# Sums written in place, an earlier place for joint product 2, joint product 4 for four column pairs, and a new timetable for the sequence sums

## The chip, the cores and the metric

One core of one Trainium2 chip. TensorE (PE) multiplies, VectorE (DVE) and ScalarE (ACT) do the elementwise work, SyncE (SP) and GpSimd (POOL) issue transfers. The metric is the device time of one execution in microseconds (us).

## The reference

Two results of one input x (2048 x 512) are mixed row by row with a sigmoid gate: a Fourier mixing over both axes, and a gated MLP with ReLU.

```python
def reference(A_x, dft_seq_re, dft_seq_im, dft_hid_re, dft_hid_im, W_gate, W_up, W_down, gate_w):
    g = sigmoid((x * gate_w).sum(-1, keepdims=True))
    a = einsum("bsd,ed->bse", x, dft_hid_re)
    b = einsum("bsd,ed->bse", x, dft_hid_im)
    y = einsum("ts,bse->bte", dft_seq_re, a) - einsum("ts,bse->bte", dft_seq_im, b)
    gate, up = x @ W_gate, x @ W_up          # 512 -> 1792 columns
    h = gate * (gate > 0) * up
    return g * y + (1 - g) * (h @ W_down)
```

## The kernel before

All products are in fp32, made of three fp32r matmuls each (high part by low part, low by high, high by high, the `PARTS`), 128x128 weights against 512 columns. Each 2x2 block product is a Strassen-Winograd scheme of seven products, numbered 1 to 7; the sums it needs are made by DVE, ACT makes high parts and copies out of PSUM, DVE makes low parts. In a tile's name the last letter tells the part: `xh`/`xl` and `wah`/`wal` are a high and a low part. The buffers' names in the profile have lost their numbers.

The stages on PE, in order: **gate and up** (the two start pairs of columns c = 0, 1, then c = 2, then the `Joined` pairs c = 3 to 6; 0 to about 233 us), the spectral blocks with the rest of gate and up, **Down** (two halves q of the rows, 347 to 481 us), and the **sequence stage** (26 products in the order `TURN`, each with four parts, to the end). A pair c does both row halves q = 0 and q = 1. Its seven block products use four PSUM banks x, m, y, t (`BANK`).

In `Joined` pairs product 2 (and from pair `FOURS` on product 4 too) is not made for each q on its own. `JointW` makes both q at once with seven products of a quarter of the size each ("joint product 2" and "joint product 4"; `step(y)` is three matmuls). Its steps stand between the block products, at the places that the dictionaries `slots` (joint product 2, called `joint`) and `fours` (joint product 4, called `self.four`) name: after block product m, half i. Joint product 2 gathers its results in bank x, joint product 4 in bank t; DVE and ACT bring them to `jo`, and their partial results to `jv`, `jv6`. A q's results are finished as sums (`added`, `last`): a DVE sum of PSUM and SBUF into a buffer `u`, then a `h`, the product of its rectified first half with its second half, and `h` goes to DRAM (`hd`), for some blocks with further sums `hs` (`h_sums`), for those in `RAW` without them (then `Down.made` makes them later, from the loaded blocks).

No order is written down for the other engines. Every operation is recorded with a key, a place in PE's count of matmuls, and `Plan.order` lists DVE, ACT, SP and POOL by it, from estimated times. Each engine then works strictly in its list's order, so an instruction that waits holds back all behind it. SBUF is 51 units of 4 KB per partition (`UNITS`). A buffer takes a unit whose former owner is done by the plan; on the chip its first writer waits until the last reader of the former owner, an engine or a transfer, has ended.

In the sequence stage `walk` and `Sequence.sides` decide when operands (`r` on the right, `l` on the left) are loaded and summed, split into `ch`, `cl` and `wh`, `wl`; the lead of each step before its use is `LEAD`, with a start ramp `RAMP`. Some operands (`FORMED`) are summed ahead of that stage: `form_stored` by POOL transfers DRAM to DRAM (`td`), the second of which adds, `form_rights` by DVE with loads and stores of SP (`rt`). The outputs' sums are `js`.

All instructions are recorded by one line of a helper, so every row of the profile says L267.

Of the kernel before, what the change touches and what calls it, by code (L numbers as in the profile page):

```python
# [11 lines left out]
OP = mybir.AluOpType  # L12
# [6 lines left out]
NT, KD, KF = S // N, D // P, F // P  # L19
HD = D // 2  # L20
UNITS = 51
FOURS, FOUR_KEY, FOUR_W = 4, -100, 40

# [29 lines left out]
        (25, 1), (0, -1), (4, -1)),  # L55
}

FORMED = (16, 18, 19, 28, 35, 37, 38)
DRAWN = {39: 38, 33: 16, 41: 19, 31: 2, 29: 15, 20: 15, 27: 7, 25: 7, 21: 6, 40: 9, 43: 9}
FLIP_T, FLIP_K = (1, 1, -1, -1), (1, 1, 1, 1)  # L60
LFORMED = (8, 9, 10, 11, 14, 15, 20, 21)
# [2 lines left out]
DIRECT, PLACE = (9, 10, 11, 14, 15, 20, 21), (0, 2, 3, 1)  # L64
GROUP = {9: 1, 10: 0, 11: 1, 14: 1, 15: 0, 20: 0, 21: 0}
ROOM = {'r': 6, 'l': 4}
LEAD = {'r': {'load': 56, 'sum': 56, 'sums': 8, 'draws': 30, 'hi': 42, 'lo': 34}, 'l': {'load': 40, 'sum': 46, 'sums': 8, 'draws': 56, 'hi': 55, 'lo': 48}}
RAMP = 50
FORM_LEAD = 43


def walk(side, blocks, room, ready=(), drawn={}):
# [197 lines left out]
class Plan:  # L270
# [14 lines left out]
    def op(self, key, f, *a):  # L285
        self.ops.append((key, len(self.ops), f, a))
# [135 lines left out]
def kernel(ctx: ExitStack, tc, xP, xG, wgu, wd, cr, ci, wri, gw, out):  # L422
# [24 lines left out]
    plan = Plan()  # L447
    op, pe = plan.op, plan.pe
# [6 lines left out]
    od = Buf(plan, "od", (NT, P, KD, N), kind="dram", tile=out)  # L455
    td = hbm("td", len(FORMED), 2, 2, P, 2, N)
    gd = hbm("gd", 2, NT * KD, P)
# [8 lines left out]
    def buf(name, shape=(2, N), dtype=F32):  # L466
        return Buf(plan, name, list(shape), dtype)
# [21 lines left out]
    def E():  # L489
        return plan  # L490
# [118 lines left out]
    FORM = {1: 0, 2: 1, 3: 2, 5: 3, 7: 4, 6: 5, 4: 6}  # L609


    RAW = {(0, 1), (1, 2), (0, 0), (0, 3), (0, 2), (1, 3)}

    def h_sums(q, c, h, key):
        f = [buf(f"hs{n}") for n in range(2)]
# [19 lines left out]
    def h_out(q, c, h, key):  # L635
        if (q, c // 2) not in RAW:
            h_sums(q, c, h, key)
        op(key + 2, lambda: put(hd[q, 0, :, c], h[0][:, 0]))
        op(key + 3, lambda: put(h_forms(q, c, 1), h[1].all))
        if (q, c // 2) in RAW:  # L640
            op(key + 2, lambda: put(hd[q, 3, :, c], h[0][:, 1]))

    class Block:


        def __init__(self, q, w, banks=PAIRS):
            self.q, self.w, self.banks = q, w, banks
            self.x = {m: X[q, m] for m in ORDER if (q, m) in X}
            self.g = {r: buf("g" + r, (N,)) for r in ("11", "21")}
            self.s = {m: buf(f"s{m}") for m in (5, 6)}  # L650
            self.u = {r: buf("u" + r) for r in ("12", "22")}
            self.h = [buf(f"h{d}") for d in range(2)]

        def run(self):
# [48 lines left out]


        def added(self, r, a, b, key):
            u, h = self.u[r], self.h[int(r[0]) - 1][:, int(r[1]) - 1]
            op(key, lambda: E().vector.tensor_add(u.all, a.all, b.all))
            op(key + 1, lambda: E().vector.scalar_tensor_tensor(h, u[:, 0], 0.0, u[:, 1], op0=OP.max, op1=OP.mult))

    class Joined(Block):  # L710


        def __init__(self, q, w, four=None):
            super().__init__(q, w)
            self.four = four
            if four and q:
                self.banks = {**PAIRS, "y": PAIRS["t"]}
            self.u["11"] = buf("u11")
            if four:
                self.u["21"] = buf("u21")  # L720
            if not q:
                self.s[1] = buf("s1")

        def run(self, joint=None):
            slots = {(5, 1): (5, 1), (6, 1): (6,), (3, 0): (3, 7), (3, 1): (2, 4)}
            order = [(3, 0), (7, 0), (3, 1), (7, 1), (4, 0), (4, 1)]
            fours = {}
            if self.four:
                slots = {(5, 1): (5, 1), (6, 1): (6,), (7, 0): (3, 7), (3, 0): (2, 4)}
                fours = {(6, 0): (5, 1), (7, 0): (6,), (7, 1): (3, 7), (3, 0): (2, 4)}  # L730
                order = [(7, 0), (7, 1), (3, 0), (3, 1)]
            for m, i in [(m, i) for m in (1, 5, 6) for i in range(2)] + order:
                pe(6, self.product, m, i)
                if m == 6 or m == 7 and not self.four:
                    self.half(m, i, plan.now)
                if i:
                    self.evac(m, plan.now)
                for j, some in ((self.four, fours), (joint, slots)) if joint else ():
                    for y in some.get((m, i), ()):
                        j.step(y)  # L740
                        if j is self.four and y == 4:
                            self.last(plan.now)
                if self.four and not joint and (m, i) == (7, 1):
                    self.last(plan.now)

        def last(self, key):
            u, y, o = self.u["21"], self.banks["y"], self.four.o[self.q]
            op(key + 1, lambda: E().vector.tensor_sub(u.all, y.all, o.all))
            op(key + 2, lambda: E().vector.scalar_tensor_tensor(
                self.h[1][:, 0], u[:, 0], 0.0, u[:, 1], op0=OP.max, op1=OP.mult))  # L750

        def done(self, key, joint):
            self.added("11", self.s[1] if self.q == 0 else self.banks["x"], joint.o[self.q], plan.now)
# [330 lines left out]
    class Down(Round):  # L1084
# [10 lines left out]
        def rights(self):  # L1095
            for (x, jj), key in self.at.items():
                if (self.q, jj) not in RAW:
                    raw = buf("hr")
# [27 lines left out]

    PAIRED = {v: n for n, v in enumerate(FORMED)}

# [6 lines left out]
    def formed(side, blocks, trails, parts, first, last, source, name, shape):  # L1135
# [4 lines left out]
        for part, trail in chains:  # L1140
            old = None
            for x, v in trail:
                b = buf(name, shape)
                op(key - FORM_LEAD, lambda b=b, x=x, part=part: load(b.all, source(part, x)))
                if old:
# [15 lines left out]
    def form_rights(values, first, last):  # L1161
        formed("r", 16, trails("r", 16, values), range(4), first, last, right_of, "rt", (2, N))
# [10 lines left out]
    def form_stored(values, first, gap):  # L1173

        for n, (v, part) in enumerate((v, part) for v in values for part in range(4)):
            a, b, _ = SUMS["r"][v - 16]
            if PACED:
                token(first + gap * 2 * n)
            for i, (f, x) in enumerate(((store, a), (accumulate, b))):
                op(first + gap * (2 * n + i), lambda f=f, x=x, v=v, part=part: f(right_of(part, v), right_of(part, x), max_dma_last_dim=8 * N))  # L1180

    def form_lefts(values, first, last):
        formed("l", 8, trails("l", 8, values), (0, 2), first, last, left_of, "lt", (4, HD))

    class Sequence:
# [8 lines left out]
        def ready(self, turn, part):  # L1194

            key = self.at(turn, part)
            return key - max(0, RAMP - (key - self.base) / 2)

# [66 lines left out]
        def run(self):  # L1265
            lead = LEAD["r"]
            llead = LEAD["l"]

            r = self.sides("r", 16, FORMED, DRAWN, (2, N), right_of, range(4), lead)
            l = self.sides("l", 8, LFORMED, LDRAWN, (4, HD), left_of, (0, 2), llead)  # L1270
# [253 lines left out]
    for n, m in enumerate((5, 6, 3, 7, 4)):  # L1524
        key = 24 * n + 20
        for f, *a in ((x_sum(0, m),), (hi_of, X[0, m]), (lo_of, X[0, m])):
            op(key, f, *a)
        for w in ws:
# [3 lines left out]
            else:  # L1532
                h, i = divmod(SLOT[m], 2)
# [16 lines left out]
    for b in start:  # L1550
        b.done(plan.now + 8)

    form_stored([16, 35, 37, 18], 156, 22)
    form_rights([28, 38], 864, 1253)


    spectral = Spectral()
# [6 lines left out]
    for c in range(2, NP):  # L1564
# [10 lines left out]
        else:  # L1575
            if c == FOURS:
                four_x = JointFour(plan.now + FOUR_KEY)
            four = c >= FOURS and JointW(w, four_x, plan.now + FOUR_W, 4)
# [26 lines left out]
    key = plan.now  # L1605
# [4 lines left out]
    for n in range(2):  # L1610
# [2 lines left out]
            op(key + k + 6 * n, lw.sum, m, n)  # L1613
        for m, k in ((5, -90), (6, 10), (3, 48), (7, 88), (2, 130), (4, 170)):
            lw.split(m, n, key + k + 14 * n, 8)
    form_stored([19], plan.now + 20, 25)
    Down(lw, 0)
    form_lefts([8], plan.now + -129, plan.now + 104)
    Down(lw, 1)

    Sequence().run()
# [54 lines left out]
```

## Time and profile before

| | us |
|---|---|
| median of 3 runs (768.67 to 772.97) | 770.83 |
| the profiled execution's own time | 769.49 |
| its span, first to last instruction | 767.7 |
| PE busy (3357 matmuls) | 762.1 |
| DVE busy | 677.7 |
| ACT busy | 407.8 |

The granted clock was 1.00 throughout. The profile is of one execution, 1.34 us quicker than the median; 1.8 us of its own time lie outside the span. Sums of durations are made against 769.49 and then carried to the median.

### The profile page before, as it was taken

What the parts mean: (1) busy time and instruction counts of PE and PEld (TensorE: products, weight loads), DVE (VectorE), ACT (ScalarE), POOL (GpSimd) and SP (SyncE); (2) the same over time, 40 slices, a digit from 0 to 9 for tenths busy, and PEclk for the clock granted to TensorE, in tenths of its full rate; (3) what the DMA queues carried; (4) which work ended last, traced back from release to release, by engine and by line L of the source; (5) the groups of instructions that cost most, each with busy time, mean ns of one, the idle gap of its engine ahead of it and who ended that gap; (6) DMA issues with size and microseconds to landing.
All of it is one profiled execution on the core that took longest, in us unless ns stands there. A gap on an engine that the chain in (4) does not pass through costs nothing.

```text
span 767.7 us, 9404 instructions
## 1 busy us (share of the span) xinstructions
PE 762.1 (99%) x3357; PEld 627.4 (82%) x3357; DVE 677.7 (88%) x757; ACT 407.8 (53%) x497; POOL 95.0 (12%) x118
## 2 busy tenths in 40 slices
PE   9999999999999999999999999999999999999998
PEld 7788888788788888888888888888888888888886
DVE  6999787867699885999999869998989999979987
ACT  5766454343444452656644536645674556827633
POOL 0111211112000000003510000130210210113010
PEclk9999999999999999999999999999999999999999
DMA  9385887758698999989599798998995998989984
GB/s 320 120 218 125 223 256 203 217 142 222 186 319 302 365 403 365 371 307 323 150 242 369 257 410 310 285 242 168 327 261 174 255 254 278 242 198 281 298 191 109
DMA packets 65503, 197.51 MB, mean 257 GB/s; under 512 B 6960, under 2 KB 7472, under 8 KB 65456
## 3 DMA queue, kind: packets, MB, share of 16 engines
q1 hardware_dynamic: 51776, 147.49, 52.8%
q0 software_dynamic: 13536, 49.29, 32.2%
q8 instruction: 26, 0.43, 0.2%
q14 instruction: 21, 0.17, 0.1%
q10 hardware_dynamic: 144, 0.13, 0.1%
HBM read 149.68 MB, written 68.17 MB: 284 GB/s over the span
## 4 chain that ended last, share of the span: by engine, by line
PE 88%; DVE 7%; DMA 2%; issue 2%; ACT 1%; DVEq 0%; ACTq 0%
PE ps L267 88%; DVE cl L267 2%; DVE u L267 1%; DVE r L267 1%; DMA hd<-h 1%; DMA hd<-hs 1%; DVE wl L267 1%; DVE h L267 1%; DVE js L267 0%; ACT ch L267 0%; DVE jws L267 0%; DVE wb1l L267 0%; DVE jw L267 0%; DVE jo L267 0%; DVE ps L267 0%
## 5 line engine op out<-in xcount | busy, mean ns | idle before, releaser
L267 PE MATMUL ps<-ch,wl 128*128 128x512 f32 (+1 forms) x420 | 162.7, 387 | 0.1
L267 PE MATMUL ps<-cl,wh 128*128 128x512 f32 (+1 forms) x420 | 162.7, 387 | 0.0
L267 PE MATMUL ps<-ch,wh 128*128 128x512 f32 (+1 forms) x420 | 162.5, 387 | 0.0
L267 ACT CAST ch<-r 128x1024 fp32r<-128x1024 f32 x104 | 105.3, 1052 | 95.2 <-DVE r L267 83.0
L267 DVE TENSOR_TENSOR cl<-r,ch 128x1024 fp32r<-128x1024 f32 x104 | 124.3, 1221 | 3.8 <-ACT ch L267 3.2
L267 PEld LDWEIGHTS ps<-ch,wl 128*128 128x128 f32 x420 | 78.9, 188 | 16.6 <-DVE js L267 0.5
L267 PEld LDWEIGHTS ps<-cl,wh 128*128 128x128 f32 x420 | 78.9, 188 | 16.6 <-DVE cl L267 0.4
L267 PEld LDWEIGHTS ps<-ch,wh 128*128 128x128 f32 x420 | 78.9, 188 | 15.9
L267 PE MATMUL ps<-ch,ll 128*128 128x512 f32 x196 | 76.2, 389 | 0.0
L267 PE MATMUL ps<-cl,lh 128*128 128x512 f32 x196 | 76.2, 389 | 0.0
L267 PE MATMUL ps<-ch,lh 128*128 128x512 f32 x196 | 76.2, 389 | 0.0
L267 ACT CAST ch<-hr 128x1024 fp32r<-128x1024 f32 (+1 forms) x56 | 51.0, 944 | 36.7 <-DVE hr L267 22.7
L267 ACT COPY s<-ps 128x1024 f32<-128x1024 f32 (+1 forms) x48 | 41.7, 874 | 50.1 <-PE ps L267 38.8
L267 DVE TENSOR_TENSOR cl<-hr,ch 128x1024 fp32r<-128x1024 f32 (+1 forms) x56 | 59.4, 1087 | 6.8 <-ACT ch L267 5.4
L267 POOL COPY tk<-tk 128x1 f32<-128x1 f32 x20 | 23.0, 1152 | 250.3 <-ACT tk L267 250.3
L267 ACT CAST wh<-l 128x1024 fp32r<-128x1024 f32 x38 | 39.5, 1053 | 16.3 <-DVE l L267 13.0
L267 DVE TENSOR_TENSOR wl<-l,wh 128x1024 fp32r<-128x1024 f32 x38 | 46.0, 1220 | 0.3 <-ACT wh L267 0.2
L267 PE MATMUL ps<-xh,wb0l 128*128 128x512 f32 x112 | 43.8, 391 | 0.0
L267 PE MATMUL ps<-vh,xl 128*128 128x512 f32 x112 | 43.7, 390 | 0.0
L267 PE MATMUL ps<-xl,wb0h 128*128 128x512 f32 x112 | 43.6, 389 | 0.0
L267 PE MATMUL ps<-xh,wb1l 128*128 128x512 f32 x112 | 43.6, 389 | 0.0
L267 PE MATMUL ps<-vh,xh 128*128 128x512 f32 x112 | 43.6, 389 | 0.0
(161 smaller groups left out, 1502.9 us busy)
## 6 DMA issues: line engine op xcount, KB each, us to landing
l<-ad SPq DMA_DIRECT2D x32, 512.0 KB, 7.5
hr<-hd SPq DMA_DIRECT2D x30, 512.0 KB, 6.0
r<-td SPq DMA_DIRECT2D x24, 512.0 KB, 7.4
td<-cr POOLq DMA_DIRECT2D x20, 512.0 KB, 5.2
td<-ci POOLq DMA_DIRECT2D x20, 512.0 KB, 6.0
wr<-wgu SPq DMA_DIRECT2D x16, 512.0 KB, 7.5
ad<-a SPq DMA_DIRECT2D x16, 512.0 KB, 7.4
r<-cr SPq DMA_DIRECT2D x16, 512.0 KB, 6.8
```

What stands on the lines that cost most here:

```text
L267: getattr(getattr(nc, self.engine), self.name)(*map(ap, self.a), **{k: ap(x) for k, x in self.k.items()})
```

## The change

Eight edits. (1) Sums that went to buffers `u` are written over one of their operands (`s5`, `s6`, `jo`). (2) Joint product 2's steps 2 and 4 stand right after joint product 4's steps 3 and 7, before the whole of block product 3. (3) `FOURS` is 3 instead of 4, so joint product 4 is made for pairs 3 to 6, and the keys of its operands differ. (4) `RAW` holds other blocks. (5) to (8) Other operands are summed ahead (`FORMED`), at other times, and the leads of the sequence stage differ.

```diff
--- before.py
+++ after.py
@@ -19,7 +19,7 @@
 NT, KD, KF = S // N, D // P, F // P
 HD = D // 2
 UNITS = 51
-FOURS, FOUR_KEY, FOUR_W = 4, -100, 40
+FOURS, FOUR_KEY, FOUR_W = 3, 0, 35
 
 
 
@@ -55,7 +55,7 @@
         (25, 1), (0, -1), (4, -1)),
 }
 
-FORMED = (16, 18, 19, 28, 35, 37, 38)
+FORMED = (16, 17, 18, 19, 35, 37, 38)
 DRAWN = {39: 38, 33: 16, 41: 19, 31: 2, 29: 15, 20: 15, 27: 7, 25: 7, 21: 6, 40: 9, 43: 9}
 FLIP_T, FLIP_K = (1, 1, -1, -1), (1, 1, 1, 1)
 LFORMED = (8, 9, 10, 11, 14, 15, 20, 21)
@@ -64,9 +64,9 @@
 DIRECT, PLACE = (9, 10, 11, 14, 15, 20, 21), (0, 2, 3, 1)
 GROUP = {9: 1, 10: 0, 11: 1, 14: 1, 15: 0, 20: 0, 21: 0}
 ROOM = {'r': 6, 'l': 4}
-LEAD = {'r': {'load': 56, 'sum': 56, 'sums': 8, 'draws': 30, 'hi': 42, 'lo': 34}, 'l': {'load': 40, 'sum': 46, 'sums': 8, 'draws': 56, 'hi': 55, 'lo': 48}}
-RAMP = 50
-FORM_LEAD = 43
+LEAD = {'r': {'load': 46, 'sum': 60, 'sums': 4, 'draws': 30, 'hi': 42, 'lo': 26}, 'l': {'load': 38, 'sum': 62, 'sums': 6, 'draws': 40, 'hi': 51, 'lo': 34}}
+RAMP = 80
+FORM_LEAD = 56
 
 
 def walk(side, blocks, room, ready=(), drawn={}):
@@ -609,7 +609,7 @@
     FORM = {1: 0, 2: 1, 3: 2, 5: 3, 7: 4, 6: 5, 4: 6}
 
 
-    RAW = {(0, 1), (1, 2), (0, 0), (0, 3), (0, 2), (1, 3)}
+    RAW = {(0, 1), (0, 0), (1, 1), (0, 3), (0, 2), (1, 0), (1, 3)}
 
     def h_sums(q, c, h, key):
         f = [buf(f"hs{n}") for n in range(2)]
@@ -648,7 +648,6 @@
             self.x = {m: X[q, m] for m in ORDER if (q, m) in X}
             self.g = {r: buf("g" + r, (N,)) for r in ("11", "21")}
             self.s = {m: buf(f"s{m}") for m in (5, 6)}
-            self.u = {r: buf("u" + r) for r in ("12", "22")}
             self.h = [buf(f"h{d}") for d in range(2)]
 
         def run(self):
@@ -703,9 +702,9 @@
 
 
         def added(self, r, a, b, key):
-            u, h = self.u[r], self.h[int(r[0]) - 1][:, int(r[1]) - 1]
-            op(key, lambda: E().vector.tensor_add(u.all, a.all, b.all))
-            op(key + 1, lambda: E().vector.scalar_tensor_tensor(h, u[:, 0], 0.0, u[:, 1], op0=OP.max, op1=OP.mult))
+            h = self.h[int(r[0]) - 1][:, int(r[1]) - 1]
+            op(key, lambda: E().vector.tensor_add(b.all, a.all, b.all))
+            op(key + 1, lambda: E().vector.scalar_tensor_tensor(h, b[:, 0], 0.0, b[:, 1], op0=OP.max, op1=OP.mult))
 
     class Joined(Block):
 
@@ -715,9 +714,6 @@
             self.four = four
             if four and q:
                 self.banks = {**PAIRS, "y": PAIRS["t"]}
-            self.u["11"] = buf("u11")
-            if four:
-                self.u["21"] = buf("u21")
             if not q:
                 self.s[1] = buf("s1")
 
@@ -726,7 +722,7 @@
             order = [(3, 0), (7, 0), (3, 1), (7, 1), (4, 0), (4, 1)]
             fours = {}
             if self.four:
-                slots = {(5, 1): (5, 1), (6, 1): (6,), (7, 0): (3, 7), (3, 0): (2, 4)}
+                slots = {(5, 1): (5, 1), (6, 1): (6,), (7, 0): (3, 7), (7, 1): (2, 4)}
                 fours = {(6, 0): (5, 1), (7, 0): (6,), (7, 1): (3, 7), (3, 0): (2, 4)}
                 order = [(7, 0), (7, 1), (3, 0), (3, 1)]
             for m, i in [(m, i) for m in (1, 5, 6) for i in range(2)] + order:
@@ -744,10 +740,10 @@
                     self.last(plan.now)
 
         def last(self, key):
-            u, y, o = self.u["21"], self.banks["y"], self.four.o[self.q]
-            op(key + 1, lambda: E().vector.tensor_sub(u.all, y.all, o.all))
+            y, o = self.banks["y"], self.four.o[self.q]
+            op(key + 1, lambda: E().vector.tensor_sub(o.all, y.all, o.all))
             op(key + 2, lambda: E().vector.scalar_tensor_tensor(
-                self.h[1][:, 0], u[:, 0], 0.0, u[:, 1], op0=OP.max, op1=OP.mult))
+                self.h[1][:, 0], o[:, 0], 0.0, o[:, 1], op0=OP.max, op1=OP.mult))
 
         def done(self, key, joint):
             self.added("11", self.s[1] if self.q == 0 else self.banks["x"], joint.o[self.q], plan.now)
@@ -1550,8 +1546,9 @@
     for b in start:
         b.done(plan.now + 8)
 
-    form_stored([16, 35, 37, 18], 156, 22)
-    form_rights([28, 38], 864, 1253)
+    form_stored([19, 35, 37], 181, 22)
+    form_stored([18], 810, 26)
+    form_rights([17, 38], 906, 1367)
 
 
     spectral = Spectral()
@@ -1613,9 +1610,9 @@
             op(key + k + 6 * n, lw.sum, m, n)
         for m, k in ((5, -90), (6, 10), (3, 48), (7, 88), (2, 130), (4, 170)):
             lw.split(m, n, key + k + 14 * n, 8)
-    form_stored([19], plan.now + 20, 25)
+    form_stored([16], plan.now + 112, 34)
     Down(lw, 0)
-    form_lefts([8], plan.now + -129, plan.now + 104)
+    form_lefts([8], plan.now + -149, plan.now + 98)
     Down(lw, 1)
 
     Sequence().run()
```

The first place is on PE, at the end of row half q = 0 of pair 4. `kx` are joint product 4's operands, `jx` joint product 2's (`jx2`, `jx4` for its steps 2 and 4); `xh3`, `xl3` with `wb1` are block product 3, `xh1` with `wal` is the first product of q = 1. Before:

```order
L267 MATMUL ps_76<-kx4_960,wd_1416 128x512 x3
L267 MATMUL ps_76<-jx2_665,wal_1311 128x512
L267 MATMUL ps_76<-jx2_665,wah_1284 128x512 x2
L267 MATMUL ps_76<-jx4_714,wal_1311 128x512
L267 MATMUL ps_76<-jx4_714,wah_1284 128x512 x2
L267 MATMUL ps_76<-xh3_209,wb1l_1348 128x512
L267 MATMUL ps_76<-xl3_278,wb1h_1335 128x512
L267 MATMUL ps_76<-xh3_209,wb1h_1335 128x512
L267 MATMUL ps_76<-xh3_209,wb1l_1348 128x512
L267 MATMUL ps_76<-xl3_278,wb1h_1335 128x512
L267 MATMUL ps_76<-xh3_209,wb1h_1335 128x512
L267 MATMUL ps_76<-xh1_312,wal_1311 128x512
```

Now:

```order
L267 MATMUL ps_76<-kx7_877,jw_1369 128x512 x3
L267 MATMUL ps_76<-jx2_658,wal_1295 128x512
L267 MATMUL ps_76<-jx2_658,wah_1249 128x512 x2
L267 MATMUL ps_76<-jx4_706,wal_1295 128x512
L267 MATMUL ps_76<-jx4_706,wah_1249 128x512 x2
L267 MATMUL ps_76<-xh3_209,wb1l_1358 128x512
L267 MATMUL ps_76<-xl3_278,wb1h_1303 128x512
L267 MATMUL ps_76<-xh3_209,wb1h_1303 128x512
L267 MATMUL ps_76<-xh3_209,wb1l_1358 128x512
L267 MATMUL ps_76<-xl3_278,wb1h_1303 128x512
L267 MATMUL ps_76<-xh3_209,wb1h_1303 128x512
L267 MATMUL ps_76<-xh4_361,wd_1388 128x512
```

Joint product 2's last six matmuls stood between joint product 4's last three and the second half of block product 3, six matmuls before q = 1's first. Now they stand ahead of the whole of block product 3, and 18 matmuls lie between: both its halves (12) and joint product 4's last six, of which the last row is the first.

The second place is on DVE and ACT, at the start of pair 3 (q = 0). DVE before, from the sum of product 7 on:

```order
L267 TENSOR_TENSOR u_749<-ps,s_657 128x1024
L267 TENSOR_TENSOR jw<-jws,jw 128x512
L267 TENSOR_TENSOR ws_759<-wr_612,wr_624 128x512
L267 TENSOR_TENSOR ws_759<-wr_612,ws_682 128x512
L267 TENSOR_TENSOR u_773<-ps,s_678 128x1024
L267 SCALAR_TENSOR_TENSOR h_782<-u_749 128x512
L267 TENSOR_TENSOR wb1l<-ws_759,wb1h 128x1024
L267 SCALAR_TENSOR_TENSOR h_731<-u_773 128x512
```

Now, from the same sum on, here in place in `s`; `kx` and the second `jws` and `jw` are operands of joint product 4, which pair 3 did not have:

```order
L267 TENSOR_TENSOR s_650<-ps,s_650 128x1024
L267 TENSOR_TENSOR h_730<-g_684,ps 128x512
L267 TENSOR_TENSOR wb0l<-ws_673,wb0h 128x1024
L267 TENSOR_TENSOR s_669<-ps,s_669 128x1024
L267 TENSOR_TENSOR jw<-jws,jw 128x512
```

```order
L267 TENSOR_TENSOR jx_706<-jx_666,jx_706 128x512
L267 TENSOR_TENSOR ws_761<-wr_603,wr_615 128x512
L267 TENSOR_TENSOR ws_761<-wr_603,ws_673 128x512
L267 TENSOR_TENSOR kx_772<-xs_634,xs_354 128x512
L267 SCALAR_TENSOR_TENSOR h_776<-ps,g_758 128x512
L267 TENSOR_TENSOR jws<-wr_615 128x128
L267 TENSOR_TENSOR jws<-jws,wr_615 128x128
L267 TENSOR_TENSOR jws<-wr_615 128x128
L267 TENSOR_TENSOR jws<-wr_615,jws 128x128
L267 TENSOR_TENSOR kx_780<-kx_772,kx_780 128x512
L267 SCALAR_TENSOR_TENSOR h_776<-s_650 128x512
L267 TENSOR_TENSOR wb1l<-ws_761,wb1h 128x1024
```

The low part `wb1l` is the 7th row from the sum of product 7 before and the 17th now, four of them with 128 columns. And ACT, with its waits, before:

```order
L267 ACTIVATE ps_76<-ps_76 128x1024 [waits PE_49]
L267 CAST jw_747<-jws_720 128x512 [waits DVE_49,Activation_49]
L267 COPY tk_75<-tk_75 128x1
L267 CAST wb1h_770<-ws1_759 128x1024 [waits DVE_49,PE_49]
L267 ACTIVATE g21_779<-ps_76 128x512 [waits PE_49,Activation_49]
L267 COPY s1_793<-ps_76 128x1024 [waits PE_49]
```

Now:

```order
L267 CAST jw_740<-jws_711 128x512 [waits DVE_49,Activation_49]
L267 ACTIVATE g21_758<-ps_76 128x512 [waits PE_49,Activation_49]
L267 CAST wb1h_769<-ws1_761 128x1024 [waits DVE_49,Activation_49]
L267 CAST kx5_780<-kx0_772 128x512 [waits DVE_49]
L267 CAST jw_804<-jws_784 128x512 [waits DVE_49,Activation_49]
L267 COPY tk_75<-tk_75 128x1
L267 COPY s1_816<-ps_76 128x1024 [waits DVE_49,PE_49,Activation_49]
```

The copy `s1` (the first product of q = 0 out of bank y) waited for PE alone; now it waits for DVE too: its unit was that of `ws1_761`, whose last reader is `wb1l`.

The third place is on DVE in the sequence stage, from the sum `js` on that waits for the end of a turn (687.65 us in the profile). Before:

```order
L267 TENSOR_TENSOR cl_5652<-r_5154,ch_5641 128x1024
L267 TENSOR_TENSOR r_5178<-r_5438,r_5178 128x1024
L267 TENSOR_TENSOR cl_5669<-r_5562,ch_5626 128x1024
L267 TENSOR_TENSOR cl_5678<-r_5178,ch_5666 128x1024
L267 TENSOR_TENSOR l_5685<-l_5588,l_5593 128x1024
L267 TENSOR_TENSOR r_5200<-r_5465,r_5200 128x1024
L267 TENSOR_TENSOR wl_5703<-l_5685,wh_5693 128x1024
L267 TENSOR_TENSOR cl_5714<-r_5579,ch_5648 128x1024
L267 TENSOR_TENSOR cl_5723<-r_5200,ch_5709 128x1024
```

Now, from the same place in the stage on:

```order
L267 TENSOR_TENSOR cl_5600<-r_5106,ch_5589 128x1024
L267 TENSOR_TENSOR l_5607<-l_5516,l_5520 128x1024
L267 TENSOR_TENSOR cl_5616<-r_5512,ch_5570 128x1024
L267 TENSOR_TENSOR r_5129<-r_5391,r_5129 128x1024
L267 TENSOR_TENSOR wl_5634<-l_5607,wh_5614 128x1024
L267 TENSOR_TENSOR cl_5644<-r_5533,ch_5623 128x1024
L267 TENSOR_TENSOR cl_5653<-r_5129,ch_5638 128x1024
L267 TENSOR_TENSOR r_5152<-r_5415,r_5152 128x1024
L267 TENSOR_TENSOR js_5597<-js_5597,ps_76 128x1024
L267 TENSOR_TENSOR cl_5673<-r_5152,ch_5665 128x1024
```

The last row of each is the low part that the first matmul of the next turn's part 3 needs. Ahead of each piece stand seven rows from that `js` on, which are the same in both. So 15 rows lay from the start of `js` to the start of this low part before, and 16 now: the sum `js_5597`, which followed the low part before (as `js_5656`), has moved ahead of it.

## Rows read from the trace of the kernel before

**Rows 1.** The page, busy time, share of the span and instructions of each engine.
```profile
PE 762.1 (99%) x3357; PEld 627.4 (82%) x3357; DVE 677.7 (88%) x757; ACT 407.8 (53%) x497; POOL 95.0 (12%) x118
```

**Rows 2.** Windows, core 0: stretch, length, busy time (instructions) of each engine, clock, DMA.
```profile
120.00:140.00 20.00, 19.21 (x85) 15.59 (x84) 12.75 (x21) 7.57 (x13) 2.68 (x5) 1.00 0.77 201
...
440.00:460.00 20.00, 20.00 (x90) 16.57 (x89) 12.32 (x11) 5.66 (x6) 0.00 (x0) 1.00 1.02 406
```

**Rows 3.** Timeline of PE at four pauses: start, time of the piece, instruction [idle before].
```profile
133.56 0.84 PE L267 MATMUL ps<-jx,jw 128*128 128x512 f32 x3
135.19 0.96 PE L267 MATMUL ps<-jx,jw 128*128 128x512 f32 x3 [0.79 <-ACT jv L267]
135.99 0.40 PE L267 MATMUL ps<-xh,wb1l 128*128 128x512 f32 x1
...
143.96 0.39 PE L267 MATMUL ps<-xh,wb1h 128*128 128x512 f32 x1
144.40 0.50 PE L267 MATMUL ps<-xh,wal 128*128 128x512 f32 x1
...
203.15 0.39 PE L267 MATMUL ps<-xh,wb0h 128*128 128x512 f32 x1
203.90 0.74 PE L267 MATMUL ps<-kx,jw 128*128 128x512 f32 x2 [0.36 <-DVE jw L267]
...
644.67 0.39 PE L267 MATMUL ps<-ch,wh 128*128 128x512 f32 x1
645.14 0.50 PE L267 MATMUL ps<-ch,wl 128*128 128x512 f32 x1
```

**Rows 4.** Chain of waits around these pauses: start, duration, what.
```profile
127.92 6.56 DMA hd<-hs
...
134.56 0.59 ACT jv L267
...
143.76 0.60 ACT jo L267
...
182.18 7.88 DMA hd<-h
```

**Rows 5.** Timeline of DVE, ACT and PE, 76 to 94 us (start of pair 3).
```profile
76.44 0.29 DVE L267 TENSOR_TENSOR jws<-wr 128x128 f32<-128x128 f32 x1
...
77.37 0.68 DVE L267 TENSOR_TENSOR h<-g,ps 128x512 f32<-128x512 f32 x1
...
79.70 1.22 DVE L267 TENSOR_TENSOR u<-ps,s 128x1024 f32<-128x1024 f32 x1
80.84 0.68 DVE L267 TENSOR_TENSOR jw<-jws,jw 128x512 fp32r<-128x512 f32 x1
81.44 0.69 DVE L267 TENSOR_TENSOR ws<-wr,wr 128x512 f32<-128x512 f32 x1
...
77.32 1.01 ACT L267 ACTIVATE ps<-ps 128x1024 f32<-128x1024 f32 x1 [0.86 <-PE ps L267]
...
85.48 1.02 ACT L267 COPY s<-ps 128x1024 f32<-128x1024 f32 x1 [1.11 <-PE ps L267]
...
89.36 0.39 PE L267 MATMUL ps<-xh,wb0l 128*128 128x512 f32 x1
```

**Rows 6.** Timeline of DVE, then PE, 686 to 716 us (sequence stage).
```profile
687.65 1.22 DVE L267 TENSOR_TENSOR js<-js,ps 128x1024 f32<-128x1024 f32 x1 [4.04 <-PE ps L267]
...
704.20 2.35 DVE L267 TENSOR_TENSOR cl<-r,ch 128x1024 fp32r<-128x1024 f32 x2
...
706.73 0.40 PE L267 MATMUL ps<-cl,wh 128*128 128x512 f32 x1
```

**Rows 7.** DMA of 177 to 196 us, then 200 to 205 us: queue rows, issues (landing time last).
```profile
q0 software_dynamic: 626, 2.24, 57.2%
...
q1 hardware_dynamic: 397, 0.78, 41.6%
...
hd<-h SPq DMA_DIRECT2D x1, 512.0 KB, 2.8
```

## The prediction

> **What bounds the kernel now.** I read the page's busy times first. TensorE is busy 99% of the span with 3357 matmuls [rows 1]; 762.1 / 3357 gives 0.227 us for each. So two things are worth time here: matmuls that go, and pauses of TensorE that go or come. Next I read the windows for the pauses: a full stretch of 20 us holds 90 matmuls and one with pauses fewer, 85 between 120 and 140 us [rows 2]. Then I read the timeline of PE where the count is low. The reader is to see starts further apart than 0.23 us per matmul. From 133.56 to 135.19 three matmuls should take 0.68 and took 1.63 us, a pause of 0.95; the next three took 0.80, so refilling cost another 0.12 [rows 3]. I add that 0.11 or so to each pause below. Last I read in the chain of waits who was late at each.
>
> The Trainium skill ("Perfetto Trace Analysis", Identifying the Most-Contended Engine) calls matmul busy time a bad measure of how near TensorE is to its limit, and asks for the weight loads' share instead. That share is 82% here, and by it DVE with 88% would be the engine to look at; I come back to it among the rivals.
>
> **Matmuls removed.** Pair 3 now takes joint product 4: seven steps of three matmuls in place of four halves of six, 21 for 24. That is 3 x 0.227 = 0.68 us less. Nothing else on PE changes in number.
>
> **Pauses removed.** (a) 134 us, 1.07 us. The copy `jv` started at 134.56, when the store `hd<-hs`, 6.56 us long, had landed [rows 4]: its unit had been that of `hs`. Now its unit comes from an `h`, stored several us before it is wanted, and the `hs` of this pair is gone (`RAW` holds block (1, 1)). (b) 144 us, 0.44 - 0.23 + 0.11 = 0.32 us. The first matmul of q = 1 writes bank x, and started when the copy `jo` (143.76, 0.60 us) had emptied it [rows 3, 4]. With 18 matmuls, 4.1 us, between joint product 2's last step and this matmul, in place of 6 (1.4 us), the copy is done early. The same pause stands once more at 181 us (0.33 us) and goes for the same reason. What is moved ahead of is joint product 4's last steps: they come six matmuls later than joint product 2's, in a bank of their own, and their sums have block product 3's second half as cover. (c) 203 us, 0.75 - 0.23 + 0.11 = 0.63 us, a wait for DVE's `jw` [rows 3]. DVE was late there because from 182.18 on its `wal` had waited 7.88 us for the store of an `h` [rows 4]. That store ran while POOL's stored sums held 57.2% of the DMA engines; with none of them in a stretch, the same kind of store took 2.8 us [rows 7]. By the new keys POOL's first batch ends at key 181 + 22 x 23 = 687, about 160 us, and the next starts at 810, some 184 us or later, mostly after this store. (d) 645 us, 0.47 - 0.23 + 0.11 = 0.35 us, where `js` comes late [rows 3]: between the preceding sum that waits for PE and this one DVE's list is three instructions shorter. Together 1.07 + 0.32 + 0.33 + 0.63 + 0.35 = 2.70 us.
>
> The sentence of the Trainium skill on this ("DMA: Bandwidth & Descriptors", Issuing engines are not separate DMA queues) is that transfers of SP and GpSimd run on the same 16 engines and interleave; the two stores of (c) agree with it.
>
> **Pauses added.** (e) Start of pair 3. ACT's copy `s1` empties bank y for block product 6, whose first matmul starts at 89.36; before, it waited for PE alone and ran at 85.48 [rows 5]. Now it takes the unit of `ws1`, so it waits for `wb1l`. What is queued ahead of that on DVE: the sum of product 7 starts when ACT's copy of bank t ends (77.32 + 1.01, about 78.40), then three instructions of 1024 columns at 1.14 apart (79.70 to 80.84), nine of 512 at 0.60 (80.84 to 81.44), and four `jws` in 0.93 (76.44 to 77.37) [rows 5]. 3.42 + 5.40 + 0.93 = 9.75, so `wb1l` starts at 88.15 and ends 1.22 later, at 89.37. The copy takes 1.02 and some 0.04 on either side: 90.47, and TensorE is 1.1 us late. Behind the copy on ACT stands the cast of `wd`, and the low part that waits for it is another 0.1 us late for joint product 4's first step. 1.2 us in all, lowest 0 (if DVE gains 1.1 us on this count), highest 2.1 (if each of the twelve wide instructions ahead starts only when the one before has ended, 1.22 for 1.14 and 0.68 for 0.60). That a sum is written in place costs nothing by itself: the one at 687.65 took 1.22 us, as the other at 79.70 did [rows 5, 6]. (f) 707 us. `js` at 687.65 waits for PE, with DVE idle for 4.04 us before it, so it can't come earlier now. The low part that part 3's first matmul (706.73) needs was the second of the two at 704.20 and ended at 706.55, a spare of 0.17 [rows 6]. One more instruction of 1024 columns ahead of it, 1.14 us: 1.0 us late. The next place where DVE's lists are compared has more instructions gone than come, so I don't carry it on. Lowest 0, highest 1.1.
>
> **Costed at nothing.** The sums in place take as many DVE instructions as before. By count DVE gets six more of 1024 columns, four more of 128 and four fewer of 512: 6 x 1.14 + 4 x 0.23 - 4 x 0.60 = 5.4 us. Most of it are sums for Down's q = 1, and their cover is DVE's idle time there: it is busy 12.32 of 20 us between 440 and 460 [rows 2]. Without the cover they would cost up to 5.4. SP issues nine transfers fewer, POOL as many as before at other times; the loads of sums stored early are wanted hundreds of us later. The other `LEAD`s move loads within the sequence stage, where PE's only pause above 0.2 us before its last part is (d). Pair 5's copy `jv6` now waits for a store of `hs`, without a pause if that lands in 2.9 us, counted along DVE's list from the pair's last sums to `hs` and along PE's from there to the step that needs the copy. It runs between POOL's batches, so I take the 2.8 us of the undisturbed row [rows 7]; with 6.56 [rows 4] it would cost 3.7.
>
> **Sum.** -0.68 - 2.70 + 1.2 + 1.0 = -1.2 us. 769.49 becomes 768.3 for an execution like the profiled one. The median lies 1.34 us above that execution, so I forecast 770.83 - 1.2 = 769.6 us.
>
> **Rivals.** *No new pause.* (e) and (f) rest on counts that a microsecond of DVE's slack undoes; without them it is -3.4 us, 767.5. *The stores stay late (slower).* If POOL's traffic still overlaps them, `jv6` in pair 5 costs 3.7 us, and `wal` of pair 6 another 2.2 at 7.88 us, its store being free up to about 5.7 by the same count: 770.83 - 1.2 + 5.9 = 775.5, or 773.3 with the first alone. The point from which it decides is a landing of 2.9 + 1.2 = 4.1 us for that `hs`. For it speak 6.56 and 7.88 [rows 4], against it the keys and 2.8 [rows 7]. *DVE is the bound.* Then its 5.4 us are all added: 770.83 - 1.2 + 5.4 = 775.0. Against it speak its idle 4.04 us ahead of a wait for PE and the 12.32 of 20 [rows 2, 6]. The page on trace analysis would say this one by its 82% against 88%; the rows with starts 0.227 us apart say that TensorE has no such reserve. *The early steps free nothing.* If bank x is late for another reason, the two pauses of (b) stay: +0.65, 770.2.
>
> **How the numbers follow.** Chances: the forecast 0.55, no new pause 0.2, late stores 0.1, DVE the bound 0.04, the early steps free nothing 0.11. The forecast's own range is 768.5 to 770.7, with the added pauses at half and at one and a half times their size. Half a per cent, 3.85 us, is what a measurement of this kernel can tell: the runs shown differ by 4.3 us. Under 767.0 lie, by that spread, two fifths of "no new pause" and a little of the forecast: 0.10. Over 774.7 lie half of the late stores and most of DVE's case: 0.07. The rest, 0.83, is no difference. The range that leaves out these ends is 766.4 to 773.3.
>
> **What would show it.** Matmuls 3354. In the timeline of PE no pause at 134, 144, 181 and 203 us (some us earlier or later by what came before), one of about 1.1 us before the first `xh,wb0l` after joint product 2's first six matmuls of pair 3, near 89.4 us, with ACT's copy `s` released by DVE `wb1l`; one of about 1 us near 706 us, with DVE's `cl` as the releaser. Wrong would be a pause in pair 5 or 6 that a store ends, a `cl` that comes in time at 706, or new pauses in the sequence stage from loads that the other leads bring too late.

## The result, and the profile after

The changed kernel is slower: 774.18 us against 770.11 (medians of 17 runs each), ratio 1.0047, 95% interval 1.0035 to 1.0059. The ratio, here and below, is estimated from all runs, so it is not just that of the two medians (1.0053). The forecast was 769.6, with a range of 766.4 to 773.3, and no difference. Its runs also lie further apart, 769.66 to 776.50 against 768.49 to 772.97. The profiled execution took 772.72 us, span 770.9, one of its quicker ones.

The page of the changed kernel, busy times:

```profile
PE 760.6 (99%) x3354; PEld 626.0 (81%) x3354; DVE 682.6 (89%) x763; ACT 408.9 (53%) x496; POOL 84.7 (11%) x118
```

Windows, columns as in [rows 2]:

```profile
100.00:120.00 20.00, 17.79 (x79) 14.40 (x78) 16.30 (x23) 7.21 (x10) 2.64 (x5) 1.00 0.69 189
120.00:140.00 20.00, 20.00 (x90) 16.57 (x89) 11.91 (x21) 8.57 (x16) 3.61 (x8) 1.00 0.70 169
140.00:160.00 20.00, 18.44 (x81) 14.94 (x81) 16.97 (x24) 7.81 (x11) 1.74 (x4) 1.00 0.67 195
440.00:460.00 20.00, 20.00 (x90) 16.57 (x89) 15.89 (x16) 7.70 (x9) 0.00 (x0) 1.00 1.02 405
```

The stretch 120 to 140, which had 85 matmuls [rows 2], is full. Two others are not: 79 and 81. The timeline of PE shows the pauses:

```profile
88.66 0.61 PE L267 MATMUL ps<-jx,wah 128*128 128x512 f32 x2
90.38 0.50 PE L267 MATMUL ps<-xh,wb0l 128*128 128x512 f32 x1 [1.11 <-ACT s L267]
...
114.85 0.39 PE L267 MATMUL ps<-xh,wb0h 128*128 128x512 f32 x1
117.45 0.50 PE L267 MATMUL ps<-xh,wb1l 128*128 128x512 f32 x1 [2.21 <-ACT s L267]
...
154.09 0.39 PE L267 MATMUL ps<-xh,wb0h 128*128 128x512 f32 x1
156.04 0.50 PE L267 MATMUL ps<-xh,wb1l 128*128 128x512 f32 x1 [1.56 <-ACT s L267]
...
708.80 0.39 PE L267 MATMUL ps<-ch,wl 128*128 128x512 f32 x1
709.65 0.50 PE L267 MATMUL ps<-cl,wh 128*128 128x512 f32 x1 [0.46 <-DVE cl L267]
```

Counted as the prediction counts (start to start, less 0.227, and 0.11 for the refill), these are 1.38, 2.48, 1.83 and 0.73 us; a smaller one at 706.17 adds 0.17. The first is the forecast's (e), the last and the one at 706.17 are its (f). The two of 2.48 and 1.83 us, together 4.31, stand in no term of it. The pauses at 134, 144, 181 and 203 us [rows 3] are gone, the one at 645 has shrunk to 0.07 us (at 647 now, without the refill).

The chain of waits before the pause at 115 us:

```profile
104.20 9.28 DMA wr<-wgu
113.47 0.02 issue
113.50 0.70 DVE ws L267
114.20 0.02 issue
114.22 0.70 DVE ws L267
114.93 0.02 issue
114.95 0.02 ACT wb0h L267
114.97 0.93 issue
115.90 1.50 ACT s L267 x2
```

The second weight load of the next pair is issued at 104.20 and lands 9.28 us later. DVE's `ws` waits for it, ACT's cast `wb0h` for `ws`, and behind `wb0h` in ACT's list stand the copies `s5` and `s6`, which need no weights at all. `s6` empties the bank that product 7 of the pair still running writes next. The chain at 154 us is the same, with a load of 8.54 us. At 115 us the list is new: in the kernel before ACT had `s5`, `s6`, `s6` and then `wb0h` at this place, so the copies ran at 109.28 to 112.6 and a weight load of 7.5 us (the longer of the two in the last line) cost TensorE nothing. ACT's timeline of before, and the landing of its weight loads there:

```profile
109.28 1.02 ACT L267 COPY s<-ps 128x1024 f32<-128x1024 f32 x1 [0.65 <-PE ps L267]
110.70 0.59 ACT L267 COPY s<-ps 128x512 f32<-128x512 f32 x1 [0.40 <-PE ps L267]
112.00 0.59 ACT L267 COPY s<-ps 128x512 f32<-128x512 f32 x1 [0.72 <-PE ps L267]
113.04 1.05 ACT L267 CAST wb0h<-ws 128x1024 fp32r<-128x1024 f32 x1 [0.36 <-DVE ws L267]
...
DMA to landing us min/median/max: 3.2/5.3/7.5
```

This is ACT's order at the end of pair 3, of before:

```order
L267 CAST wah_979<-wr0_920 128x1024 [waits DMAHW2_49,DVE_49]
L267 COPY s5_985<-ps_76 128x1024 [waits PE_49]
L267 COPY s6_994<-ps_76 128x512 [waits PE_49,Activation_49]
L267 COPY s6_994<-ps_76 128x512 [waits PE_49]
L267 COPY tk_75<-tk_75 128x1
L267 CAST wb0h_1018<-ws0_999 128x1024 [waits DVE_49]
```

And of the changed kernel:

```order
L267 COPY tk_75<-tk_75 128x1
L267 CAST wb0h_995<-ws0_986 128x1024 [waits DVE_49]
L267 COPY s5_1002<-ps_76 128x1024 [waits PE_49]
L267 COPY s6_1012<-ps_76 128x512 [waits PE_49,Activation_49]
L267 COPY s6_1012<-ps_76 128x512 [waits PE_49]
```

At 154 us the list had `wb0h` first before, too, and there the chain was close. Before's timelines of ACT and PE at that place:

```profile
149.90 1.05 ACT L267 CAST wb0h<-ws 128x1024 fp32r<-128x1024 f32 x1 [0.47 <-DVE ws L267]
150.85 1.49 ACT L267 COPY s<-ps 128x1024 f32<-128x1024 f32 x2
...
152.69 0.39 PE L267 MATMUL ps<-xh,wb1l 128*128 128x512 f32 x1
```

The copy ended at 152.34, a spare of 0.35 us. That load had been issued 11.7 us before TensorE's need and landed in at most 7.3; now it is issued 10.9 us before and lands in 8.54. 0.8 + 1.2 or more, less the spare, is the 1.7 us that came (1.83 with the refill).

### The profile page after: what moved, and what is told of

It reads as the page before. It is cut to its first block, busy times and chain, and to the rows that moved or that the text cites. A ratio compares the mean times of both kernels' runs of the same rounds, so it can differ in the third digit from the quotient of the medians.

```text
span 770.9 us, 9384 instructions
## 1 busy us (share of the span) xinstructions
PE 760.6 (99%) x3354; PEld 626.0 (81%) x3354; DVE 682.6 (89%) x763; ACT 408.9 (53%) x496; POOL 84.7 (11%) x118
## 4 chain that ended last, share of the span: by engine, by line
PE 91%; DMA 3%; DVE 3%; issue 1%; ACT 1%; SPq 0%; DVEq 0%; ACTq 0%
PE ps L267 91%; DMA wr<-wgu 2%; DMA x<-xP 1%; DVE cl L267 1%; DVE jo L267 0%; DVE r L267 0%; ACT s L267 0%; DVE ws L267 0%; DVE js L267 0%; SPq L267 0%; ACT ch L267 0%; DVE l L267 0%; DVE h L267 0%; DVE wl L267 0%; ACT xh L267 0%
## 5 line engine op out<-in xcount | busy, mean ns | idle before, releaser
L267 POOL COPY tk<-tk 128x1 f32<-128x1 f32 x20 | 11.8, 592 | 291.3 <-ACT tk L267 291.3
L267 PE MATMUL ps<-xh,wb0h 128*128 128x512 f32 x112 | 43.6, 389 | 0.0
L267 PE MATMUL ps<-xh,wb1h 128*128 128x512 f32 x112 | 43.6, 389 | 0.0
```

What stands on the lines that cost most here:

```text
L267: getattr(getattr(nc, self.engine), self.name)(*map(ap, self.a), **{k: ap(x) for k, x in self.k.items()})
```

## The experiments

**Theory.** The lost time is two things meeting: a weight load that lands 8 to 9 us after its issue because POOL's transfers share the DMA engines, and an ACT list that has `wb0h` ahead of copies TensorE waits for. **Rivals.** The sequence stage's new plan loses it; or DVE has too much to do with joint product 4 in pair 3; or the load is late by its issue or for a unit.

The first four runs take the halves of the change apart, and then each of the theory's two parts away.

**r1_gateup**, the kernel before with edits 1 to 4:

```diff
-FOURS, FOUR_KEY, FOUR_W = 4, -100, 40
+FOURS, FOUR_KEY, FOUR_W = 3, 0, 35
...
+                slots = {(5, 1): (5, 1), (6, 1): (6,), (7, 0): (3, 7), (7, 1): (2, 4)}
```

> The kernel before with the gate and up edits alone (sums in place, earlier steps of joint product 2, joint product 4 for four pairs, RAW); the sequence stage's plan as before. Theory (weight loads): the changed kernel lost its time where the second weight load of the next pair landed 8.5 to 9.3 us after its issue and ACT's list had the cast wb0h, which waits for it, ahead of the copies s5 and s6, so these edits alone should be slower than before by 2 to 4 us, with pauses of TensorE that a copy s ends near 115 and 154 us, where wb0h stands ahead of s5, and none at 645. Rival (sequence plan): the time was lost by the new plan of POOL's transfers and leads; then this kernel is 2 to 3.4 us faster than before, with neither pause.

Measured: 772.00 us, ratio 1.0035 (1.0020 to 1.0051). At 115.6 us a pause of 2.6 us, behind a load of 9.3; none at the end of pair 4, where `wb0h` stands first too but the load landed in 5.0 us. So a loss comes with these edits alone, and the list alone makes no pause. The pause (e) is there as well (1.38 us at 89). A pause of 1.56 us at 478 us, in Down, is new, behind DVE's `cl`; it is not in the changed kernel.

**r2_seq**, the kernel before with the other edits:

```diff
-RAMP = 50
-FORM_LEAD = 43
+RAMP = 80
+FORM_LEAD = 56
...
-    form_stored([16, 35, 37, 18], 156, 22)
-    form_rights([28, 38], 864, 1253)
+    form_stored([19, 35, 37], 181, 22)
+    form_stored([18], 810, 26)
+    form_rights([17, 38], 906, 1367)
```

> The kernel before with the sequence stage's edits alone (FORMED, form_stored, form_rights, form_lefts, LEAD, RAMP, FORM_LEAD). Theory (weight loads): the pause at 645 us (0.35) goes, one of 0.9 near 707 comes, the pauses of before at 134, 144, 181 stay, so within 1 us of before (same). Rival (sequence plan): 3 to 5 us slower than before.

Measured: 769.49 us, ratio 1.0003 (0.9991 to 1.0015). That rival falls. Its profile has the pauses at 144 and 181 of [rows 3] still, and (f) at 704.7 and 707.6. The pause at 134 is gone, though it was expected to stay, and three came that were not expected: 0.48 and 0.77 us at 616 and 619, behind `cl`, and 1.18 us at 118.5. The last is a late weight load once more, by another way: it lands in 9.20 us, and behind it in DVE's list `jws` comes late, then ACT's `jw`, `wb1h` and the copy that TensorE needs. So these edits too can make a weight load later (7.5 us before), and `wb0h` is not the only instruction that passes this on to TensorE.

**r3_late5**, the changed kernel with another estimate in the planner, which moves the lists and no load:

```diff
-                s.end = line + self.LANDING + (2.0 if "accum_op" in s.k else 0)
+                s.end = line + self.LANDING + (2.0 if "accum_op" in s.k else 0) + (5.0 if s.writes[0].base.name.startswith("wr") and s.key > 400 else 0)
```

> The changed kernel, with the planner told that weight loads from pair 4 on land 5 us later than it assumed. The loads themselves stay where they are; ACT's cast wb0h is then listed after the copies s5 and s6 (and DVE's ws after what does not need the load). Theory (weight loads, list order): the pauses at 115 (2.5 us) and 154 (1.8 us) go although the load lands as late as before, so 4 to 6 us faster than the changed kernel's median of 774.2, at 768.5 to 770, and a spread of its runs of 3 us in place of 7. Rival (DVE has too much to do with joint product 4 in pair 3): the pauses stay, 773 to 775.

Measured: 777.02 us, slower still (1.0089, 1.0074 to 1.0103), so the number missed. But the two pauses were gone. New ones of 1.2 and 4.0 us (without the refill) stood at 327 and 331 us, in the spectral stage, whose two weight loads the edit also concerned, and after them the granted clock was 0.50 in the stretch 335 to 338 us. r5_late5b narrows the edit.

**r4_poollate**, the changed kernel with POOL's first batch out of the stage:

```diff
-    form_stored([19, 35, 37], 181, 22)
+    form_stored([19, 35, 37], 1030, 20)
```

> The changed kernel with POOL's first batch of stored sums (values 19, 35, 37) moved from key 181 to key 1030, behind the gate and up stage; ACT's list keeps wb0h ahead of s5 and s6. Theory (the load is long because it shares the DMA engines with POOL's transfers): the second weight load of pairs 4 and 5 lands in 3 to 5 us, the pauses at 115 and 154 us go, 768.5 to 771 unless POOL's moved transfers cost something later. Rival (the load is late by its issue, or waits for a unit): it lands as late, and the pauses stay, 773 to 775.

Measured: 804.66 us. As a version it fails: behind the gate and up stage the batch meets full DMA engines. For the theory it is the other half. These are the windows of its gate and up stage and the DMA issues of 100 to 120 us, last number the landing:

```profile
100.00:120.00 20.00, 20.00 (x89) 16.40 (x88) 19.52 (x27) 7.93 (x10) 0.00 (x0) 1.00 0.30 106
140.00:160.00 20.00, 20.00 (x89) 16.39 (x88) 19.48 (x29) 8.55 (x11) 0.00 (x0) 1.00 0.28 102
```

```profile
wr<-wgu SPq DMA_DIRECT2D x2, 512.0 KB, 3.2
```

In the changed kernel the same row says

```profile
td<-ci POOLq DMA_DIRECT2D x4, 512.0 KB, 5.7
wr<-wgu SPq DMA_DIRECT2D x2, 512.0 KB, 6.8
```

(6.8 is the median of the two loads, of 4.3 and 9.28 us). Without POOL's transfers the load lands in 3.3 us and TensorE has no pause above 0.1 us at either place, though ACT's list still has `wb0h` first: the load was long by its company. The later issue cost nothing where the load was short: at the second place it stood 10.8 us before TensorE's need, against 10.9 in the changed kernel.

**r5_late5b**, r3's edit for pairs 4 to 6 alone:

```diff
... and s.key > 400
... and 400 < s.key < 900
```

> As r3_late5, but the planner is told of the later landing only for the weight loads of pairs 4 to 6; those of the two blocks in the spectral stage, whose lists r3_late5 moved too, with pauses of 1.2 and 4.0 us at 327 and 331 us, are planned as in the changed kernel. Theory (weight loads, list order): no pause at 115 and 154 us, none above 0.2 in the spectral stage, and 4 to 6 us faster than the changed kernel: 768 to 770.5, no difference to before, with the runs within 3 us of each other. Rival (moving the lists anywhere in the stage costs what it gains): 772 or more.

Measured: 769.26 us (768.83 to 770.83, 12 runs), against before 0.9995 (0.9984 to 1.0005). By the two ratios to before, 0.9995 / 1.0047, it is 0.5% or 4.0 us quicker than the changed kernel. At 115 us the load landed as late, 8.7 us after its issue, and TensorE did not stop. ACT's timeline between 109 and 117 us:

```profile
112.63 1.02 ACT L267 COPY s<-ps 128x1024 f32<-128x1024 f32 x1 [0.71 <-PE ps L267]
114.04 0.59 ACT L267 COPY s<-ps 128x512 f32<-128x512 f32 x1 [0.40 <-PE ps L267]
115.35 0.59 ACT L267 COPY s<-ps 128x512 f32<-128x512 f32 x1 [0.72 <-PE ps L267]
115.83 1.05 ACT L267 CAST wb0h<-ws 128x1024 fp32r<-128x1024 f32 x1
```

The copies wait for PE alone and `wb0h` comes after; r9_c3 has the same with a load of 8.4 us. At 154 us this profile shows less, as the load there landed in 5.8 us. What the list does at that place is seen in r10_gu_c3 below, whose load there landed in 8.0 us: the copies ran ahead of the late `wb0h`, and TensorE did not stop:

```profile
152.10 0.59 ACT L267 COPY s<-ps 128x512 f32<-128x512 f32 x1 [0.27 <-PE ps L267]
153.96 1.05 ACT L267 CAST wb0h<-ws 128x1024 fp32r<-128x1024 f32 x1 [1.18 <-DVE ws L267]
```

The new lists are not free: r3, r5 and r9 have a pause of 0.76 us near 166, in pair 5, which the changed kernel has not, behind DVE's `wd`. The spread of the runs fell from 6.8 to 2.0 us, which fits a landing that varies from run to run; no profile of a slower run shows it.

The next two, r7 and r8, ask which edit brings the list.

**r7_fours**, before with edit 3 alone (`FOURS`, `FOUR_KEY`, `FOUR_W`).

> The kernel before with joint product 4 in pair 3 too (FOURS, FOUR_KEY, FOUR_W) and no other edit. ACT's list has wb0h ahead of s5 and s6 at the end of pair 3 here. Theory (weight loads): this edit brings the pause near 115 us (1 to 3 us, by the landing), so 0 to 3 us slower than before in spite of three matmuls fewer. Rival (the earlier steps or the sums in place bring it): no such pause, 0.7 us faster than before.

Measured: 777.63 us, 1.0099 (1.0082 to 1.0117), the slowest of r1, r2, r7 and r8. The pause near 115 is there, but small (0.67 us at 118, load 8.2). The larger ones I had not expected: 2.35 us at 91 (`wd` for joint product 4's first step late, DVE having pair 3's `hs` sums as well, which the changed `RAW` removes), 1.97 at 136 and 1.25 at 195, both ended by ACT's `s`. At 195 it is the theory's chain, with a load of 8.85 us; at 136 `s` waited for a store of an `h` of 7.02 us, as in [rows 4]. The size that I expected was wrong. Which of the other edits keeps edit 3 from these pauses was not run by itself.

**r8_nofours**, the changed kernel with `FOURS, FOUR_KEY, FOUR_W = 4, -100, 40`.

> The changed kernel with FOURS, FOUR_KEY and FOUR_W as before: joint product 4 for three pairs; all other edits are in. ACT's list has s5 and s6 ahead of wb0h at the end of pair 3, as before, and wb0h ahead of both at the end of pair 4. Theory (weight loads, list order): no pause at 89 and none near 115 us, one of 1 to 2 us near 154 us if the load lands 8 us or more after its issue: 769 to 772. Rival (the pause follows from the load's landing whatever the list): both pauses stay, 773 or more.

Measured: 769.53 us, 0.9993 (0.9982 to 1.0003). Nothing at 89 and 115; at 115 the load landed in 4.4 us here, so this run does not tell the list from the landing. The one pause in the stage, 1.79 us at 159, was not the expected one (the load landed in 5.1 us): DVE's `wal` waited for the store of an `h`, as in [rows 4], and the sum after it came late. The store took 6.58 us, and DVE stood idle for the last 2.4 of them.

```profile
145.83 6.58 DMA hd<-h
152.41 0.02 issue
152.43 0.69 DVE wal L267
```

The other four try what the findings point to.

**r6_lw12_45**, r5 with `FOUR_KEY, FOUR_W = 12, 45` in place of 0, 35. The second number moves `jws` and `jw` in pairs 4 to 6 too, not in pair 3 alone.

> As r5_late5b, and joint product 4's operands of pair 3 planned 12 (kx) and 10 (jws, jw) matmuls later, so that the copy s1 at the start of pair 3 waits for PE alone again. Theory (as in the prediction, e): the pause of 1.38 us at 89 us goes and nothing takes its place: 1.2 to 1.4 us faster than r5_late5b, 766.7 to 769. Rival: the operands come late for joint product 4's first step, and a pause of 0.5 to 1.5 us near 91 us takes its place, same as r5_late5b.

Measured: 770.59 us, 1.0014 (1.0004 to 1.0024): the rival was right. The 89 us pause went, 1.54 us at 90.4 came, now ended by `jw`, and in pair 5 stands one of 1.44 in place of 0.76, ended by `jw` too:

```profile
90.36 0.39 PE L267 MATMUL ps<-xh,wb0h 128*128 128x512 f32 x1
92.01 0.96 PE L267 MATMUL ps<-kx,jw 128*128 128x512 f32 x3 [1.26 <-DVE jw L267]
```

**r9_c3**, r5 with the shift in pair 3 alone, and a smaller one for `jw`:

```diff
-FOURS, FOUR_KEY, FOUR_W = 3, 0, 35
+FOURS, FOUR_KEY, FOUR_W = 3, 14, 35
...
-            four = c >= FOURS and JointW(w, four_x, plan.now + FOUR_W, 4)
+            four = c >= FOURS and JointW(w, four_x, plan.now + FOUR_W + 5 * (c == FOURS), 4)
```

> As r5_late5b, with joint product 4's operands planned later in pair 3 alone (kx 14 matmuls, jws and jw 5), the other pairs as in r5_late5b. DVE's list there has two sums fewer ahead of wb1l, and jw and kx5 right behind it. Theory (e, corrected: the copy s1 must not wait for wb1l, and jw must be ready by 90.7 us): the pause of 1.38 us at 89 us goes and at most 0.5 us comes back near 91; 0.9 to 1.4 us faster than r5_late5b: 768 to 768.5, 0.15 to 0.25% faster than before. Rival (r6's result holds in pair 3 too: DVE has more to do there than fits): a pause of 1 us or more near 91 us, no gain.

Measured: 768.79 us (768.20 to 770.33), 0.9985 (0.9976 to 0.9995). It beats both kernels, before by 0.15%, the changed one by 0.6% (0.9985 / 1.0047). The pause at 89 is gone; 0.5 us came back at 93, behind a `jv`. In the profiles this is 0.9 us less, the low end of what was expected; the time expected, 768 to 768.5, was missed. The gain on r5 is 0.5 us by the medians and 0.8 by the ratios, whose intervals overlap, so it is not clear of noise.

**r10_gu_c3**, edits 1 to 4 with both list corrections, but POOL's plan as before.

> The gate and up edits alone (as r1_gateup), with both list corrections: weight loads of pairs 4 to 6 planned to land later, joint product 4's operands in pair 3 later. Theory: the pauses at 89, 115, 154 us go, 2.6 us from the list of weight loads and 1.3 us from pair 3, so some 3.5 us faster than r1_gateup's 772.0: 767.5 to 769.5; the pause of 1.5 us that r1_gateup has near 478 us, in Down, is from the sums that moved there and stays. Rival: the gain is given back by waits for stores in pairs 5 and 6, 770 or more.

Measured: 776.73 us, 1.0089 (1.0075 to 1.0102): the rival. The largest pause, at 171 us, is ACT's `jv` behind a store:

```profile
166.30 6.89 DMA hd<-h
173.20 0.02 issue
173.22 1.08 ACT jv L267 x2
174.30 0.04 issue
174.35 6.66 PE ps L267 x21
```

This is the case that the prediction called late stores. r9, which differs from it by edits 5 to 8, among them the new POOL plan (its first batch ends near 160 us), has no such pause. But r1, with the old plan, has none there either, so the new lists have a part in it, which was not taken apart.

**r11_nf_late**, r8 with r5's edit.

> As r8_nofours (joint product 4 for three pairs, all other edits), with the weight loads of pairs 4 to 6 planned to land later. r8_nofours has one pause above 0.7 us in the stage, 1.68 us at 159, behind DVE's wal, which waits for the store of an h. Theory (a wait at the head of DVE's list holds all behind it): with wal listed later that pause goes, and the kernel is 1.2 to 1.8 us faster than r8_nofours, near 768. Rival: the store's wait is only moved, same as r8_nofours, 769 to 770.

Measured: 769.01 us, 0.9993 (0.9984 to 1.0003). The pause at 159 went, as the theory had it, and one of 0.68 at 241 came. The time is the rival's: by the ratios to before it is no quicker than r8.

## Why the prediction was wrong, step by step

**What bounds it**: right. The spans differ by 3.2 us; the pauses counted over the whole timeline rose by 3.7 and the matmuls' time fell by 0.7.

**Matmuls removed**, 0.68: right, 3354.

**Pauses removed**, 2.70: right in each place; at 645 us 0.07 stayed. One reading in (c) was off, without effect on the sum: 7.88 us is how long the store took, and DVE stood idle for it for 2.0.

**(e)**, 1.2: 1.38 measured, ended by `s` as said. **(f)**, 1.0: 0.90 in two pauses. For (e) the profile does not name `wb1l` as the releaser of `s`, as the prediction had it, but PE. These are rows of the changed kernel, and the last one is of r9:

```profile
87.98 1.23 DVE L267 TENSOR_TENSOR wb1l<-ws,wb1h 128x1024 fp32r<-128x1024 f32 x1
89.32 1.01 ACT L267 COPY s<-ps 128x1024 f32<-128x1024 f32 x1 [1.78 <-PE ps L267]
...
85.77 1.01 ACT L267 COPY s<-ps 128x1024 f32<-128x1024 f32 x1
```

`wb1l` ended at 89.21 and a matmul of joint product 2 at 89.27, so the time alone does not decide. r6 and r9 do: there `s1` ran at 85.77, so what it needs of PE was done by then, and the pause at 89 is gone.

**Costed at nothing**: this step failed. It went through sums, stores and the sequence stage's loads, and left out the weight loads of the gate and up stage and the order of ACT's list around them. They cost 4.31 us in the profiled execution, and -1.2 + 4.3 = 3.1 is nearly its difference, 3.2. The signs were in the trace of before: DVE was idle for 1.4 us ahead of `ws` at the end of pair 3, until this very load landed, the spare at 152.69 was 0.35 us, and the order of the changed kernel's ACT shows `wb0h` ahead of `s5`. I followed the waits of PE's instructions back by the durations and landings that the loads had had before, and did not ask what each would cost if it landed as late as the stores that I did vary. r4 shows the landing's share, r5 (at 115 us) and r10 (at 154) the list's: with either one put right the two pauses go, and r5 then stands at 0.9995 of before, where the forecast was 769.6 / 770.83 = 0.9984.

The sentence of the Trainium skill named in the prediction ("DMA: Bandwidth & Descriptors", Issuing engines are not separate DMA queues) would have pointed there too: it holds for loads as for stores, and 3.3 against 9.28 us agrees with it.

**Rivals.** Late stores: not in the changed kernel, but in r10, as said; that 774.18 lies between this rival's 773.3 and 775.5 is chance. The early steps free nothing: no, the pauses of (b) are gone. DVE the bound: no; DVE's extra sums filled 440 to 460 to 15.89 us of 20 with PE's 90 matmuls intact.

**The median.** The profiled execution was again quicker than the median, by 1.5 us; that this too is the landing of these loads fits r5's narrow spread, but no profile of a slower execution shows it. A part of it can be the clock: all eight executions above 774.3 us have a mean granted clock of 0.995 to 0.998, seven of the other nine 0.999 or 1.00, and so have r5's twelve.

Open: why the planner puts `wb0h` first at the end of pair 3 with joint product 4 there (in r7 too) and not without it (in r8 it stands between the two halves of `s6`) was not taken apart further.

## What to carry to other kernels

Where an engine runs a fixed list, look at what stands behind each instruction that waits for a transfer, and price it at the longest landing in the profile, not at the one it had last time. Here a copy that frees the bank the matmuls need next did better ahead of a cast that waits for a load, even where the plan said that the load was there. A moved list has to be read through to its end, too: r3 lost more at another place than it gained. And a change that shortens the work of the bounding engine can lose by the order in which another engine's list comes out.

## What had not been expected of the hardware

After some pauses of a few us the granted clock fell to the lower of its two levels (1.2 GHz) for 3 to 5 us: in r7 after one of 2.35 us, in r10 after 2.71 (0.60 over 174 to 178 us), in r3 after 4.1 (0.50 over 335 to 338). r7's windows:

```profile
91.00:94.00 3.00, 0.92 (x5) 0.46 (x3) 2.97 (x6) 0.46 (x3) 1.13 (x2) 0.96 0.99 128
94.00:97.00 3.00, 3.00 (x7) 2.36 (x8) 1.03 (x2) 2.39 (x4) 0.00 (x0) 0.50 0.93 292
97.00:100.00 3.00, 3.00 (x14) 2.47 (x13) 0.10 (x1) 2.22 (x5) 0.42 (x1) 0.97 0.69 272
```

Seven matmuls in 3 us in place of 14 cost 7 x 0.227 = 1.6 us on top of the pause. After the pause of 2.48 us at 115 in the changed kernel, and of 2.60 in r1, the clock stayed at 1.00, so a pause of this length can go either way. The changed kernel's executions above 774.3 us, with their lower mean clocks, may have paid this too, which no profile here shows.
